# A DFT step on eight small tiles of the TensorE array instead of full matmuls with a half-empty table

## The chip, the cores and the metric

The kernel runs on one core of a Trainium2 chip. A core has TensorE (matmuls, 128x128 array, results into PSUM banks of 512 fp32 columns), VectorE (DVE), ScalarE (ACT), GpSimd (POOL), and the DMA engines, whose transfers are issued here from SyncE (SP). The metric is the device time in microseconds (us). The kernel before takes 251.26 us, the median of three runs (250.78 to 251.49). The profile is of one further execution; its span from first to last instruction is 249.1 us.

## The reference

The input has 2048 rows (S) of 640 columns (D), in bfloat16. Two branches are mixed by a gate. Branch A is a long convolution along the rows, computed with Fourier transforms of length 4096; branch B is a mixer MLP.

```python
def _A_ref(q, k, v, shift_k, ssm_k, ssm_D):
    # k_shift: sum of four shifted copies of k times shift_k ("taps")
    kv = k_shift * v
    L = 2 * S
    kv_f = rfft(kv padded to L);  kf_f = rfft(ssm_k padded to L)
    y = irfft(kv_f * kf_f)[:S] + kv * ssm_D
    return q * y

def _B_ref(x, w1, w2, w3, w4):
    h = gelu(layernorm(x) @ w1)
    # four column groups of h shifted by 1, -1, 2, -2 rows, then
    x1 = x + hs @ w2
    return x1 + gelu(layernorm(x1) @ w3) @ w4

g = sigmoid((x * gate_w).sum(-1))
return g * a + (1 - g) * b          # x = A_q in both
```

(Written shorter than the original; what is computed is the same.)

## The kernel before

The transform of length 4096 is split into two steps. Step 1 multiplies by a small DFT matrix and leaves 128 x 2 rows per block in DRAM scratch (`S_x` for kv, `S_h` for the filter). Step 2 finishes the forward transform, `product` multiplies the two spectra as complex numbers, step 3 is the first inverse step, and step 4 the last inverse step together with the gate. Steps 2 and 3 work on 32 groups of 128 rows, four groups to a task, so there are 8 tasks for x, 8 for h, 8 products and 8 tasks of step 3.

The twiddle values of step 2 stand in a compact table `CMP[:, 0]` (128 partitions, 32 groups, 2 parts c, 32 columns). For a full 128x128 matmul they are spread into `T2`: each partition belongs to one parity j (its bit 6, that is partitions 0 to 63 or 64 to 127), and its values go into the columns of that parity; the columns of the other parity are zero. Half of `T2` is therefore zero.

```python
def scaled(ev, dst, src, a):
    if ev == "A":
        A.activation(out=dst, in_=src, func=ACT.Copy, scale=a)
    else:
        V.tensor_scalar(out=dst, in0=src, scalar1=a, scalar2=0.0, op0=ALU.mult, op1=ALU.add)

def table(which, ev):
    if "I" not in st:
        TB = main.tile([P, 2, NG, P], BF16, name="TB", tag="RT")
        st["T2"], st["I"] = TB[:, 0], TB[:, 1]
    for j in range(2):
        if which == 0:
            j and (yield)
            scaled(ev[j], st["T2"].rearrange("p g (c j k) -> p g c j k", c=2, j=2)[:, :, :, j, :], CMP[:, 0], bit(6) if j else col(8))
        else: ...                      # the same for the inverse table I

def gather(name, s):                   # four groups of scratch, 640 KB
    ax = pool("C").tile([P, 4, D], BF16, name="ax", tag="ax", bufs=3)
    ...
    SP.dma_start(out=ax[:], in_=...)

def step2(name, s, ev):
    ax = st.pop((name, s))
    dst = []
    def make(u):                       # u = 0..4: one PSUM bank of 512 columns
        box = {}
        def first():
            ps = box["ps"] = psc.tile([P, 512], F32, name="ps2", tag="c")     # ring of 4 banks
            for a, b in cuts(512 * u, 512 * u + 512):                         # cut where a group of 640 ends
                i = a // D
                PE.matmul(ps[:, a - 512 * u:b - 512 * u], lhsT=st["T2"][:, 4 * s + i, :], rhs=ax[:, i, a - i * D:b - i * D], start=True, stop=True)
        def second():
            ...                        # hs from pool "L2", tag "hp", 4 buffers, or xs from pool "C", 2 buffers
            evac(ev[u], dst[0][:].rearrange("p g d -> p (g d)")[:, 512 * u:512 * u + 512], box["ps"][:])
        return first, second
    return banks(5, make)

def product(s):
    h, x = st.pop(("hs", s)), st.pop(("xs", s))
    p2 = pool("L2").tile([P, 4, D], BF16, name="p2", tag="hp", bufs=4)
    V.tensor_tensor(out=p2[0:64], in0=x[0:64], in1=h[64:128], op=ALU.mult)
    ...                                # five VectorE operations of 2560 columns in all
```

`evac` copies a PSUM bank into SBUF on ScalarE ("A") or VectorE ("V"), letter by letter as the task's name says. Small tiles of the array are already used in two places, the gate's row and the taps:

```python
def z_rows():
    ps = psc.tile([P, 512], F32, name="psz", tag="c")
    for k in range(DC):
        for c in range(4):
            PE.matmul(ps[32 * c:32 * c + 1, :]..., lhsT=GW[:, k:k + 1], rhs=st["xt", c][:, :, k, :],
                      start=(k == 0), stop=(k == DC - 1), tile_position=(0, 32 * c))
    ...

def tap(q, ev):                        # the matmuls of its first step
            for e in range(2):
                a = slice(H * e, H * e + H)          # H = 64: two row tiles, one bank each
                PE.matmul(ps[e][:, lo:hi, :], lhsT=kt[a], rhs=st["DG"][a, 4 * k + lo - i:4 * k + hi - i, a], ...)
```

Steps 1 to 4 are interleaved with the MLP (`mlp1`, `w2`, `w3`, `w4`), whose matmuls use another ring of PSUM. Every engine's order of instructions is fixed by one long list, `ORDER`, that names task, arguments and step:

```python
ORDER = (
    "open.L1.left:0 open.A2.right:0 kv_alloc:0 load_x0.1:0 consts0:0 ..."
    ...
    "... step2.x.7.AAAAV:0 step2.x.7.AAAAV:2 scale_x1.6.V:0 step2.x.7.AAAAV:4 step2.x.7.AAAAV:1 ..."
```

Of the kernel before, what the change touches and what calls it, by code (L numbers as in the profile page):

```python
# [16 lines left out]
P = 128  # L17
S = 2048
D = 640
# [22 lines left out]
def kernel(  # L42
# [196 lines left out]
    def f4_table():  # L239

        stt(col(0), bit(1), 2.0, bit(0))
        stt(col(1), bit(2), 4.0, col(0))
        stt(col(1), col(1), -1.0, pf[:])
        ts(col(1), col(1), 0.25, 1.0)
        stt(col(1), col(0), 32.0, col(1))
# [28 lines left out]
    def i_tables():  # L274

        ts(col(12), bit(5), -1.0, 1.0)
        ts(col(18), bit(5), 2.0, 1.0)
# [4 lines left out]
        ts(ag[:], R64[:, 0:NG], 4.0, col(18))  # L282
        yield
# [15 lines left out]
    def table(which, ev):  # L299

        if "I" not in st:
            TB = main.tile([P, 2, NG, P], BF16, name="TB", tag="RT")
            st["T2"], st["I"] = TB[:, 0], TB[:, 1]
        for j in range(2):
            if which == 0:
                j and (yield)
                scaled(ev[j], st["T2"].rearrange("p g (c j k) -> p g c j k", c=2, j=2)[:, :, :, j, :], CMP[:, 0], bit(6) if j else col(8))
            else:
                j and (yield)
                scaled(ev[j], st["I"].rearrange("p g (j c k) -> p g j c k", j=2, c=2)[:, :, j], CMP[:, 1], bit(5) if j else col(12))  # L310
# [77 lines left out]
    def gather(name, s):  # L388

        ax = pool("C").tile([P, 4, D], BF16, name="ax", tag="ax", bufs=3)  # L390
# [5 lines left out]
    def step2(name, s, ev):  # L396
        ax = st.pop((name, s))
        dst = []

        def make(u):  # L400
            box = {}

            def first():
                ps = box["ps"] = psc.tile([P, 512], F32, name="ps2", tag="c")
                for a, b in cuts(512 * u, 512 * u + 512):
                    i = a // D
                    PE.matmul(ps[:, a - 512 * u:b - 512 * u], lhsT=st["T2"][:, 4 * s + i, :], rhs=ax[:, i, a - i * D:b - i * D], start=True, stop=True)  # L407

            def second():
                if not dst:  # L410
                    if name == "h":
                        dst.append(pool("L2").tile([P, 4, D], BF16, name="hs", tag="hp", bufs=4))
                    else:
                        dst.append(pool("C").tile([P, 4, D], BF16, name="xs", tag="xs", bufs=2))
                    st[name + "s", s] = dst[0]
                evac(ev[u], dst[0][:].rearrange("p g d -> p (g d)")[:, 512 * u:512 * u + 512], box["ps"][:])
# [606 lines left out]
```

## Time and profile before

| Engine | busy us | share of the span | instructions |
|---|---|---|---|
| TensorE, matmuls (PE) | 227.3 | 91% | 1637 |
| TensorE, weight loads (PEld) | 128.6 | 52% | 1637 |
| VectorE (DVE) | 212.2 | 85% | 425 |
| ScalarE (ACT) | 177.9 | 71% | 292 |
| GpSimd (POOL) | 11.3 | 5% | 26 |

The busy time of an engine is the union of its instructions' times. Matmuls overlap in the array, so the mean time of one (299 ns for step 2's) is its way through the array and not what it adds; what it adds is read from the distance of the starts. In a group's line the first shape is the stationary side (rows*columns of the array), the second the moving side. "ps<-ax,TB" is step 2 (TB holds both tables), "ps<-hs,TB" step 3; xs and hs are the spectra of kv and of the filter, p and hs on VectorE the product. The copies out of PSUM all have the line of their helper, L321 on ScalarE and L323 on VectorE.

### The profile page before, as it was taken

How to read it: one execution, taken by the hardware profiler on the slowest of the kernel's cores; microseconds unless marked ns; L12 is line 12 of the kernel's file. 1: busy time of each engine (PE TensorE's matmuls, PEld its weight loads, DVE VectorE, ACT ScalarE, POOL GpSimd, SP SyncE). 2: the span in 40 equal slices, each digit the busy share in tenths (PEclk: the TensorE clock that was granted, in tenths of full speed). 3: DMA queues.
4: the chain of work that ended last, by engine and by line, in shares of the span. 5: the costliest groups of instructions: out<-in, count | busy, mean ns of one | idle time of the engine just before them, and what ended most of it. 6: DMA issues, size and time to landing. Idle time of an engine off the chain costs nothing. (4 is left out here: it accounts for less than half of the span.)

```text
span 249.1 us, 4377 instructions
## 1 busy us (share of the span) xinstructions
PE 227.3 (91%) x1637; PEld 128.6 (52%) x1637; DVE 212.2 (85%) x425; ACT 177.9 (71%) x292; POOL 11.3 (5%) x26
## 2 busy tenths in 40 slices
PE   0746999999999999999999899999989989999994
PEld 0735564444477555444555355555544546546652
DVE  6989998549995999985899999999999997508995
ACT  5599996984699999999988958845678460144530
POOL 1003301000000100031000000000000000000000
PEclk9997999999999999999999999999999999999999
DMA  6999897968858959995997618998403953268773
GB/s 250 377 416 291 189 216 167 240 256 263 241 217 243 387 204 233 346 381 146 183 304 215 204 64 251 186 366 302 132 3 101 342 218 105 105 237 281 222 265 108
DMA packets 50980, 57.65 MB, mean 231 GB/s; under 512 B 25610, under 2 KB 42763, under 8 KB 50703
## 3 DMA queue, kind: packets, MB, share of 16 engines
q1 hardware_dynamic: 50958, 57.38, 74.5%
q8 instruction: 13, 0.21, 0.4%
q14 instruction: 9, 0.07, 0.1%
HBM read 33.77 MB, written 18.36 MB: 209 GB/s over the span
## 5 line engine op out<-in xcount | busy, mean ns | idle before, releaser
L782 PE MATMUL ps<-W,gt 128*128 128x512 bf16 (+1 forms) x384 | 56.6, 299 | 0.0
L764 PE MATMUL ps<-x1t,W 128*128 128x512 bf16 x240 | 55.1, 379 | 0.0
L782 PEld LDWEIGHTS <-gt 128*128 128x128 bf16 x384 | 30.3, 98 | 23.2 <-issue 1.1
L769 ACT ACTIVATE gt<-ps 128x1024 bf16<-128x1024 f32 x24 | 24.5, 1041 | 20.3 <-PE ps L764 20.2
L764 PEld LDWEIGHTS <-W 128*128 128x128 bf16 x240 | 23.3, 98 | 26.4 <-issue 0.3
L323 DVE CAST stg<-ps 128x512 bf16<-128x512 f32 x41 | 26.4, 683 | 5.5 <-PE ps L370 5.3
L639 PE MATMUL psm<-xt,WA 128*128 128x512 bf16 x100 | 23.4, 379 | 0.0
L407 PE MATMUL ps<-ax,TB 128*128 128x512 bf16 (+3 forms) x128 | 22.5, 299 | 0.6 <-DVE hs L323 0.4
L321 ACT CAST stg<-ps 128x512 bf16<-128x512 f32 x39 | 21.7, 602 | 1.2 <-PE ps L370 1.1
L716 PE MATMUL psw<-WA,HT 128*128 128x512 bf16 (+1 forms) x116 | 21.6, 299 | 0.0
L321 ACT CAST gs<-ps 128x512 bf16<-128x512 f32 x29 | 15.2, 599 | 7.5 <-PE ps L446 7.5
L321 ACT CAST xs<-ps 128x512 bf16<-128x512 f32 x27 | 14.7, 617 | 7.0 <-PE ps L407 5.0
L321 ACT CAST hs<-ps 128x512 bf16<-128x512 f32 x27 | 14.2, 601 | 3.2 <-PE ps L407 3.2
L407 PEld LDWEIGHTS <-TB 128*128 128x128 bf16 x128 | 11.6, 98 | 9.2 <-issue 1.9
L784 DVE SCALAR_TENSOR_TENSOR X<-ps,OMG,X 128x640 bf16<-128x640 f32 x16 | 14.0, 877 | 2.4 <-PE ps L782 2.4
L718 DVE SCALAR_TENSOR_TENSOR X<-psw,X 128x640 bf16<-128x640 f32 x16 | 13.1, 819 | 3.3 <-PE psw L716 3.3
L522 PE MATMUL psk<-DG,KT 64*128 64x256 bf16 (+3 forms) x190 | 11.1, 250 | 5.0 <-ACT yk L530 3.7
L815 DVE SCALAR_TENSOR_TENSOR q<-ps,GS,q 128x320 bf16<-128x320 f32 x15 | 7.8, 542 | 9.0 <-PE ps L805 9.0
L639 PEld LDWEIGHTS <-WA 128*128 128x128 bf16 x100 | 9.5, 98 | 11.5 <-issue 0.7
L809 ACT ACTIVATE y<-ps,GS 128x320 bf16<-128x320 f32 x17 | 8.1, 525 | 9.7 <-PE ps L805 7.3
L716 PEld LDWEIGHTS <-HT 128*128 128x128 bf16 x116 | 10.1, 98 | 9.5 <-issue 0.7
L642 ACT ACTIVATE HT<-psm 128x1024 bf16<-128x1024 f32 (+1 forms) x12 | 10.5, 888 | 6.1 <-PE psm L639 5.9
(147 smaller groups left out, 386.3 us busy)
## 6 DMA issues: line engine op xcount, KB each, us to landing
S_x<-stg SPq DMA_DIRECT2D x8, 640.0 KB, 4.3
ax<-S_x SPq DMA_DIRECT2D x8, 640.0 KB, 5.3
S_h<-stg SPq DMA_DIRECT2D x8, 640.0 KB, 9.0
ax<-S_h SPq DMA_DIRECT2D x8, 640.0 KB, 5.3
S_g<-gs SPq DMA_DIRECT2D x8, 640.0 KB, 5.7
W<-in_B_w_dram SPq DMA_DIRECT2D x2, 1920.0 KB
KV<-in_A_v_dram SPq DMA_DIRECT2D x4, 640.0 KB, 11.6
gin<-S_g SPq DMA_DIRECT2D x4, 640.0 KB, 6.5
```

The source lines that it names most:

```text
L321: A.copy(out=dst, in_=src)
L323: V.tensor_copy(out=dst, in_=src)
L407: PE.matmul(ps[:, a - 512 * u:b - 512 * u], lhsT=st["T2"][:, 4 * s + i, :], rhs=ax[:, i, a - i * D:b - i * D], start=True, stop=True)
L522: PE.matmul(ps[e][:, lo:hi, :], lhsT=kt[a], rhs=st["DG"][a, 4 * k + lo - i:4 * k + hi - i, a], start=(i == 0), stop=(i == 7))
L639: PE.matmul(ps[:, v, :].rearrange("p (a b) -> p a b", a=4), lhsT=W1N[:, k, 160 * f:160 * f + P] if f < 4 else W1M[:, k, :], rhs=xt[:, :, k ...
L642: A.activation(out=st["HT"][:, 4 * c:4 * c + 4, 2 * u:2 * u + nf, :].rearrange("p t f b -> p f t b"), in_=ps[:].rearrange("p f (t b) -> p ...
L716: PE.matmul(ps[:, o:o + w], lhsT=h_tile(f, t1), rhs=W2P[:, f, o:o + w], start=(f == 0), stop=(f == 4))
L718: V.scalar_tensor_tensor(out=X1[:, t1, :], in0=ps[:], scalar=1.0, in1=X[:, t1, :], op0=ALU.mult, op1=ALU.add, accum_out=S12[:, 0, t1:t1 + 1])
L764: PE.matmul(ps[:, u, :].rearrange("p (a b) -> p a b", a=4), lhsT=st["W3"][:, k, f * P:(f + 1) * P], rhs=xt[:, :, k, :], start=(k == 0), st ...
L769: A.activation(out=gt[:, 2 * (fp % 2):2 * (fp % 2) + 2, :], in_=ps[:], func=ACT.Gelu_apprx_tanh)
L782: PE.matmul(ps[:, o:o + w], lhsT=st["gt", c, f // 4][:, f % 4, i * P:(i + 1) * P], rhs=st["W4"][:, f, o:o + w], start=(f == 0), stop=(f == ...
L784: V.scalar_tensor_tensor(out=X1[:, t1, :], in0=ps[:], scalar=OMG[:, t1:t1 + 1], in1=X1[:, t1, :], op0=ALU.mult, op1=ALU.add)
```

## The change

Step 2 no longer uses `T2`. A matmul with 64 rows and 32 columns is placed on one of eight tiles of the array: row tile j (partitions 64j to 64j+63), column tile 64c + 32o. Two groups, o = 0 and 1, share the four column tiles, so that one set of eight small matmuls covers two groups, straight from the compact table. Each parity j has its own PSUM bank. A task therefore takes eight groups (two gathers) and fills ten banks; there are 4 tasks for x and 4 for h. The groups come out in another order, which is set right in the inverse table, in the place of step 3's results in scratch, and in the last table. The spectra of x now lie in a tile `XS` of four parts, in the place that the tables had; the fourth buffer for `ax`, and a place of its own for `p2`, come from the room that `T2` leaves. The `ORDER` of all engines, and with it the engine that each copy goes to, was drawn up anew for these tasks.

```diff
     def f4_table():
         ...
+        stt(col(1), bit(3), 2.0, col(1))
+        stt(col(1), bit(4), -2.0, col(1))
         ...
     def i_tables():
-        ts(col(18), bit(5), 2.0, 1.0)
+        ts(col(18), bit(5), 4.0, 1.0)
         ...
+        odd = ag[:].rearrange("p (i j) -> p i j", j=2)[:, :, 1]
+        ts(odd, odd, -2.0, op0=ALU.add)
     def table(which, ev):
-        (T2 and I in one tile TB; which == 0 spreads CMP[:, 0] into T2, twice)
+        st["I"] = pool("C").tile([P, NG, P], BF16, name="I")
+        for o in range(2):
+            o and (yield)
+            scaled(ev[o], st["I"].rearrange("p g (j c k) -> p g j c k", j=2, c=2)[:, :, o], CMP[:, 1], bit(5) if o else col(12))
     def gather(name, s):
-        ax = pool("C").tile([P, 4, D], BF16, name="ax", tag="ax", bufs=3)
+        ax = pool("C").tile([P, 4, D], BF16, name="ax", tag="ax", bufs=4)
-    def step2(name, s, ev):
-        ax = st.pop((name, s))
+    def step2(name, b, ev):
+        ax = [st.pop((name, 2 * b + h)) for h in range(2)]
         def make(u):
+            ps = []
             def first():
-                ps = box["ps"] = psc.tile([P, 512], F32, name="ps2", tag="c")
-                for a, b in cuts(512 * u, 512 * u + 512):
-                    i = a // D
-                    PE.matmul(ps[:, a - 512 * u:b - 512 * u], lhsT=st["T2"][:, 4 * s + i, :], rhs=ax[:, i, a - i * D:b - i * D], start=True, stop=True)
+                for j in range(2):
+                    ps.append(psc.tile([P, 512], F32, name="ps2", tag="c"))
+                for lo, hi in cuts(512 * u, 512 * u + 512):
+                    i = lo // D
+                    for o in range(2):
+                        for c in range(2):
+                            for j in range(2):
+                                q, r = H * c + 32 * o, slice(H * j, H * j + H)
+                                PE.matmul(ps[j][q:q + 32, lo - 512 * u:hi - 512 * u], lhsT=CMP[r, 0, 8 * b + 2 * i + o, c, :],
+                                          rhs=ax[i // 2][r, 2 * (i % 2) + o, lo - i * D:hi - i * D], start=True, stop=True, tile_position=(H * j, q))
-            def second():
+            def second(j):
                 ...
+                        st["XS"] = main.tile([P, 4, 4, D], BF16, name="XS", tag="RT")
+                        t = st["XS"][:, (2 * b + j) % 4]
-                evac(ev[u], dst[0][:]...[:, 512 * u:512 * u + 512], box["ps"][:])
-            return first, second
+                evac(ev[2 * u + j], dst[j]...[:, 512 * u:512 * u + 512], ps[j][:])
+            return first, lambda: second(0), lambda: second(1)
     def product(s):
-        p2 = pool("L2").tile([P, 4, D], BF16, name="p2", tag="hp", bufs=4)
+        p2 = ring.tile([P, 4, D], BF16, name="p2", tag="HM", bufs=1)
     def step3(s, ev):
-        (lhsT=st["I"][:, 4 * s + i, :]; results at 4 * s * P * D, groups side by side)
+        (lhsT=st["I"][:, 8 * (s // 2) + 2 * i + s % 2, :]; results at (8 * (s // 2) + s % 2) * P * D, every second group)
     def h_shift(c):
-        (HW and HM: two tiles)
+        (HW and HM: two parts of one tile, whose place p2 takes later)
     ORDER = (
-        ... 1034 steps
+        ... 1002 steps, all in a new order
```

## The prediction

> **What bounds the kernel now.** I read the table of engines first, then busy time in four stretches, then the groups of instructions of the third stretch, then the chain that ended last.
>
> ```profile
> PE 227.3 (91%) x1637; PEld 128.6 (52%) x1637; DVE 212.2 (85%) x425; ACT 177.9 (71%) x292; POOL 11.3 (5%) x26
> ```
>
> TensorE and VectorE are both near full on average, so neither alone is "the" bound. The stretches end where the forward transforms of step 2 begin (111.7 us), where the first product begins (123.0), where the last product ends (208.5), and at the end:
>
> ```profile
> core 0: us, PE busy (x) PEld busy (x) DVE busy (x) ACT busy (x) POOL busy (x), PEclk, DMA share, GB/s
> 0.00:111.70 111.70, 97.37 (x806) 57.44 (x807) 95.04 (x274) 95.74 (x156) 9.89 (x24) 0.98 0.87 273
> 111.70:123.00 11.30, 11.17 (x70) 6.00 (x69) 7.79 (x15) 11.27 (x19) 1.38 (x2) 1.00 0.80 167
> 123.00:208.50 85.50, 81.84 (x505) 43.40 (x503) 83.38 (x78) 58.20 (x97) 0.00 (x0) 1.00 0.69 207
> 208.50:249.10 40.60, 36.92 (x261) 21.72 (x258) 26.04 (x60) 12.69 (x22) 0.00 (x0) 1.00 0.55 187
> ```
>
> In the third stretch VectorE is busy 83.4 of 85.5 us and TensorE 81.8: TensorE has little slack there, VectorE hardly any. In the fourth TensorE alone is full. The chain says the same: VectorE from 136 to 198 us, TensorE from there to 245.
>
> ```profile
> DVE 23%; PE 18%; issue 2%; ACT 0%; ACTq 0%; DVEq 0%
> ```
>
> The groups that the change touches, over the whole span:
>
> ```profile
> L407 PE MATMUL ps<-ax,TB 128*128 128x512 bf16 (+3 forms) x128 | 22.5, 299 | 0.6 <-DVE hs L323 0.4
> L323 DVE CAST hs<-ps 128x512 bf16<-128x512 f32 x13 | 8.5, 684 | 0.2
> L323 DVE CAST xs<-ps 128x512 bf16<-128x512 f32 x13 | 8.5, 683 | 3.4 <-PE ps L407 3.4
> L297 DVE TENSOR_SCALAR TB<-CMP,BF 128x2048 bf16<-128x2048 bf16 x2 | 1.4, 746 | 0.0
> ```
>
> **What small tiles cost here.** Two parts of the kernel before already use them: the gate's row (four column tiles) and the shift taps (two row tiles). Three lines of the timeline:
>
> ```profile
> 46.31 0.81 PE L639 MATMUL psm<-xt,WA 128*128 128x512 bf16 x3
> 47.05 1.25 PE L650 MATMUL psz<-xt,GW 128*1 128x512 bf16 x20
> 48.23 0.39 PE L370 MATMUL ps<-KV,F 128*128 128x512 bf16 x1
> ```
>
> Twenty 512-column matmuls take 1.25 us to the end of the last. In the start times of the trace the first four begin within 10 ns, and the sets begin 215 to 216 ns apart, which is also the distance of two full 128x512 matmuls (median start to start 216; 162 for 384 columns, 109 for 256, 55 to 56 for 128). So one set of small tiles costs what one full matmul costs, and its weight loads disappear behind the set before. The taps show it for row tiles: two start 3 to 5 ns apart, and pairs follow each other at 106 to 109 ns for 256 columns.
>
> The same lines show a price. Three full matmuls from 46.31 on would be through the array by 46.96, but the first small one starts at 47.05; five sets would be through by 48.13, the next full one starts at 48.23. Entering and leaving a tile mode costs some 0.09 to 0.10 us each (92 to 97 ns at the nine changes in the trace that are not hidden by another wait).
>
> **What the Trainium skill says.** "TensorEngine Tiling (Array Packing)", section Key Properties: tiles load and multiply in parallel, but a change of tiling mode drains the engine. The trace agrees with both (sets of 216 ns; 92 to 97 ns a change). The same page, PSUM Bottleneck: tiling speeds up TensorE and not the emptying of PSUM. That bears on this kernel: 80 banks leave step 2 before and after, at 0.68 us on VectorE or 0.60 to 0.62 on ScalarE. The same page, Restrictions and Gotchas: row tiles may not share a PSUM bank at one time (the change gives each j its own bank), and column tiling switches the fast weight load off. For the last no run here shows a number: the gate's weights have one column, the new ones 32.
>
> **The change, part by part.**
>
> TensorE, step 2. Before: 16 tasks of 8 matmuls, two each of 512, 384, 256 and 128 columns: 2 x (216 + 162 + 109 + 56) = 1.09 us, 17.4 us in all. (The 22.5 of the group is larger because it counts each matmul's way through the array.) After: 8 tasks with the same cuts, each cut a set of eight small matmuls, so 8 x 1.09 = 8.7 us if a set costs what a full matmul costs. Saved: 8.7 us. In the changed kernel's order of instructions the sets stand in 21 unbroken runs of one to four pairs of banks, so 42 changes of mode x 0.094 = 3.9 us are added. The changed schedule also turns one more block of x through TensorE (20 transposes at 55 ns, 1.1 us). Net on TensorE: -8.7 + 3.9 + 1.1 = -3.7 us.
>
> VectorE. The forward table goes (2 x 0.746 = 1.5 us). The whole order was drawn up anew, and with it the split between VectorE and ScalarE. By kinds: two row statistics fewer (-2.3), three taps moved (-0.8), six copies of step 1 fewer (-4.1), three rows normalized more in each of the two norms (+2.6), one scaling more (+0.4), three transposed blocks emptied (an estimate from ScalarE's 1.03 and 0.63 us for the same: +3), four copies more in step 2 (30 for 26, +2.7), four fewer in step 3 (-2.7), the table (-1.5), small things +0.5. Sum: about -2 us of 212. ScalarE gains about as much.
>
> The third stretch matters more than the sum. From its first product to its last VectorE now holds 25 copies out of PSUM, 8 gated sums of the MLP, 40 product operations, 3 norms and 2 scalings: 25 x 0.683 + 8 x 0.877 + 40 x 1.487 + 2.1 = 85.7 us, and the stretch took 85.5. After it holds 16 copies, 8 sums, 40 products, 1 norm, 4 scalings: 10.9 + 7.0 + 59.5 + 2.0 = 79.4 us. TensorE's part there falls from 80.6 (by start-to-start distances) to 71.9 plus some 2.5 of mode changes. So VectorE bounds it still, at about 79.2 us.
>
> The second stretch takes that back in part. Step 2 now works two old tasks at a time, and three of the new tasks' transforms instead of three old ones stand ahead of the first product. Between the first transform and the first product: ScalarE 22.3 us, VectorE 20.4, TensorE 19.9 plus 1.5 of changes, where it was 10.9, 8.0 and 11.3. Against that the first stretch loses 7.5 us of TensorE work (83.5 for 91.0), so it should end near 104.
>
> Sum: 104.2 + 22.3 + 79.2 + 40.6 (the fourth stretch holds the same 36.1 us of TensorE work in both) = 246.3 us of span, 2.8 less than 249.1. The other way of counting, TensorE's own sum with its idle time unchanged, gives 3.7 less. I take 3.6 off the measured 251.26, as the new order was made for the new costs and may overlap the edges of the stretches: 247.6 us.
>
> **Rivals.** (a) *Small weight loads are not hidden.* Weight loads of 32 columns without the fast path might pass one by one. With 28 ns for one (an estimate from the taps, whose 64-column pairs follow each other at 24 to 28 ns with two loads between, if those two shared the time) 512 of them are 14 us, 5.6 above the 8.7: the gain on TensorE is gone, and the time stays at 249 to 253. For it: nothing in this trace loads eight tiles of 32 columns. Against: two row tiles with 128-column weights hide theirs even behind 64 columns. (b) *VectorE takes the bound wholly.* Products and copies don't shrink, TensorE's gain becomes idle time, and only the moved copies help: 248 to 250. For it: 83.4 of 85.5 us. (c) *Two banks at a time starve the ring.* Step 2 and step 3 share four PSUM banks; a unit now needs two free ones, and runs of three or four units need up to eight in turn, each freed after 0.6 to 0.7 us, while a set of 512 columns takes 0.22. TensorE would stand inside a run, where before a matmul of the MLP stood between. Worth 0.2 to 0.4 us a run, 4 to 8 us at worst, of which VectorE's bound hides most: 248 to 252. (d) *The new order is simply better*, with less idle TensorE before 40 us (26.6 busy of 40 now): 243 to 245.
>
> **Range and chances.** Central 247.6. Rivals (b) and (c) put it up to 250.8, (d) down to 244. Faster by over 2% (under 246.2) needs the full 3.7 and a better fit besides: 0.25. Slower by over 2% (over 256.3) needs serial small tiles, which the gate's row speaks against: 0.05.
>
> **What would show it.** Right: the step-2 sets start 216 ns apart for 512 columns with eight starts inside some 25 ns; 42 gaps of 0.09 to 0.10 us where runs begin and end; products from first to last in 78 to 80 us with VectorE over 97% busy; the first product later than 123 us; the last stretch near 40.6. Wrong: sets spaced wider than one full matmul (rival a), waits of step-2 matmuls for copies above 3 us in sum (rival c; 0.6 now), or a product stretch whose VectorE shows idle time over 5 us.

## Result: 242.87 us, and the profile after

The changed kernel takes 242.87 us (median of four runs, 241.75 to 244.53) where the kernel before takes 251.02 beside it: a ratio of 0.968, 95% interval 0.962 to 0.975. It is 8.2 us faster; 3.6 were predicted, and the time lies below the predicted range of 244 to 250.8 us. The profile has a span of 240.0 us for 249.1.

The engines of the changed kernel, and its four stretches, cut at the same events as those of the kernel before (columns as there):

```profile
PE 224.6 (94%) x2041; PEld 122.6 (51%) x2041; DVE 209.6 (87%) x428; ACT 176.0 (73%) x300; POOL 11.1 (5%) x26
```

```profile
0.00:99.60 99.60, 90.31 (x791) 54.81 (x791) 89.20 (x259) 90.52 (x155) 7.33 (x20) 1.00 0.90 285
99.60:120.40 20.80, 20.80 (x274) 9.03 (x274) 17.67 (x44) 19.96 (x35) 3.75 (x6) 1.00 0.89 274
120.40:199.70 79.30, 78.12 (x748) 38.62 (x747) 77.65 (x69) 51.77 (x87) 0.00 (x0) 1.00 0.66 187
199.70:240.00 40.30, 35.38 (x238) 20.20 (x235) 25.04 (x57) 13.71 (x24) 0.00 (x0) 1.00 0.62 202
```

Set beside the prediction's sum:

| stretch | before | predicted | after | TensorE idle before, after |
|---|---|---|---|---|
| to the first step-2 matmul | 111.9 | 104.2 | 99.6 | 14.3, 9.3 |
| to the first product | 11.1 | 22.3 | 20.8 | 0.1, 0.0 |
| to the last product | 85.5 | 79.2 | 79.3 | 3.7, 1.2 |
| to the end | 40.6 | 40.6 | 40.3 | 3.7, 4.9 |

(Idle is the stretch less the union of the matmuls' times in the trace. The first cut of the kernel before lies 0.2 us later than in the prediction's table.) Three stretches came out within 1.5 us. Of the 6.3 us between the predicted span (246.3) and the measured one, 4.6 are in the first, which ends before the first small tile of step 2 runs. The engine line says the same in another way: TensorE's busy time fell by 2.7 us (227.3 to 224.6), its idle time by 6.4 (21.8 to 15.4).

Step 2's groups, and a piece of TensorE's timeline with small tiles between full matmuls (start, time covered, and what ran):

```profile
L413 PE MATMUL ps<-ax,CMP 64*32 64x512 bf16 (+3 forms) x512 | 13.4, 300 | 0.1
L322 DVE CAST XS<-ps 128x512 bf16<-128x512 f32 x21 | 13.4, 683 | 3.4 <-PE ps L413 3.3
L322 DVE CAST hs<-ps 128x512 bf16<-128x512 f32 x9 | 6.1, 685 | 0.4 <-PE ps L413 0.3
```

```profile
98.63 1.03 PE L776 MATMUL ps<-x1t,W 128*128 128x512 bf16 x4
99.59 0.63 PE L413 MATMUL ps<-ax,CMP 64*32 64x512 bf16 x24
100.15 2.33 PE L776 MATMUL ps<-x1t,W 128*128 128x512 bf16 x10
102.41 0.85 PE L413 MATMUL ps<-ax,CMP 64*32 64x384 bf16 x32
103.19 2.33 PE L776 MATMUL ps<-x1t,W 128*128 128x512 bf16 x10
```

512 small matmuls are busy 13.4 us where 128 full ones were 22.5, and they wait 0.1 us in sum. By start times, the eight of a set start within 22 to 24 ns in 58 of the 64 sets (the other six are spread wider, over 62 to 382 ns), and within a run sets of 384, 256 and 128 columns are followed by the next at the distance of full matmuls (162, 109 and 56 ns). After the first set of a run the next one comes some 10 ns later than that (226 ns for 512 columns).

The chain that ended last spends most of its time on TensorE, with VectorE second:

```profile
PE 40%; DVE 32%; ACT 18%; DMA 4%; issue 4%; SPq 0%; DVEq 0%
```

This chain reaches back to the first load; that of the kernel before begins at 136 us, so the shares of the two can't be compared.

Where the 4.6 us were is seen in the first 40 us. TensorE of the kernel before, its ScalarE in the same microseconds, and then TensorE of the changed kernel (in brackets the idle time before the group and what ended it):

```profile
15.61 1.52 PE L522 MATMUL psk<-DG,KT 64*128 64x256 bf16 x32 [0.25 <-ACT KT L321]
20.20 0.27 PE L522 MATMUL psk<-DG,KT 64*128 64x256 bf16 x1 [3.07 <-ACT yk L530]
```

```profile
15.84 1.24 ACT L221 ACTIVATE CMP<-n,NPI 128x1024 bf16<-128x1024 int32 x1
16.89 0.81 ACT L608 ACTIVATE jk<-X 128x640 bf16<-128x640 bf16 x1
...
18.55 1.13 ACT L221 ACTIVATE CMP<-n,NPI 128x1024 bf16<-128x1024 int32 x1
19.59 1.53 ACT L530 CAST yk<-psk 128x512 bf16<-128x512 f32 x3
```

```profile
14.28 1.52 PE L534 MATMUL psk<-DG,KT 64*128 64x256 bf16 x32 [0.25 <-ACT KT L320]
16.05 2.01 PE L534 MATMUL psk<-DG,KT 64*128 64x256 bf16 x44 [0.24 <-ACT yk L542]
```

Before the change TensorE has filled four banks with taps and stands for 3.07 us, because ScalarE makes the table's sines (L221) and the statistics of rows (L608) before it copies the taps out (L530). After that gap the trace shows TensorE's clock at half from 21.5 to 24.9 us, which costs some 1.7 us more (an estimate, half of the 3.41 us). The changed kernel has neither. It makes both tables much later (their four sines stand at 72 to 85 us) and has the first rows' statistics done by 12.2 us. And v, with which the taps are multiplied, is there earlier: the second quarter that the first taps need lands at 14.89 us, in the kernel before at 19.24 (landings here and below are the last update of the load's semaphore in the trace).

### The profile page after: what moved, and what is told of

The parts are those of the page before. It is cut to its first block, busy times and chain, and to the rows that moved or that the text cites. A ratio compares the mean times of both kernels' runs of the same rounds, so it can differ in the third digit from the quotient of the medians.

```text
span 240.0 us, 5176 instructions
## 1 busy us (share of the span) xinstructions
PE 224.6 (94%) x2041; PEld 122.6 (51%) x2041; DVE 209.6 (87%) x428; ACT 176.0 (73%) x300; POOL 11.1 (5%) x26
## 4 chain that ended last, share of the span: by engine, by line
PE 40%; DVE 32%; ACT 18%; DMA 4%; issue 4%; SPq 0%; DVEq 0%
PE ps L776 13%; PE ps L794 8%; PE psm L651 7%; ACT stg L320 4%; DVE p L436 4%; DVE p L434 4%; ACT HT L346 3%; PE ps L369 3%; DVE X L796 3%; DVE hs L442 3%; DVE hs L440 3%; DVE hs L438 3%; ACT KT L320 3%; ACT jk L733 3%; DMA q<-in_A_q_dram 2%
## 5 line engine op out<-in xcount | busy, mean ns | idle before, releaser
L794 PEld LDWEIGHTS <-gt 128*128 128x128 bf16 x384 | 29.6, 98 | 24.1 <-issue 2.8
L776 PEld LDWEIGHTS <-W 128*128 128x128 bf16 x240 | 22.5, 98 | 27.5 <-issue 3.4
L320 ACT CAST stg<-ps 128x512 bf16<-128x512 f32 x45 | 25.1, 637 | 0.7 <-PE ps L369 0.7
L322 DVE CAST stg<-ps 128x512 bf16<-128x512 f32 x35 | 22.8, 685 | 3.1 <-PE ps L369 2.9
L320 ACT CAST gs<-ps 128x512 bf16<-128x512 f32 x33 | 17.4, 598 | 11.0 <-PE ps L456 10.0
L320 ACT CAST hs<-ps 128x512 bf16<-128x512 f32 x31 | 16.5, 615 | 2.5 <-PE ps L413 2.4
L322 DVE CAST XS<-ps 128x512 bf16<-128x512 f32 x21 | 13.4, 683 | 3.4 <-PE ps L413 3.3
L413 PE MATMUL ps<-ax,CMP 64*32 64x512 bf16 (+3 forms) x512 | 13.4, 300 | 0.1
L733 ACT ACTIVATE jk<-X 128x640 bf16<-128x640 bf16 x16 | 13.4, 834 | 0.0
L320 ACT CAST XS<-ps 128x512 bf16<-128x512 f32 x19 | 10.5, 606 | 3.1 <-PE ps L413 3.1
```

The lines of the kernel that those rows point to most:

```text
L320: A.copy(out=dst, in_=src)
L322: V.tensor_copy(out=dst, in_=src)
L413: PE.matmul(ps[j][q:q + 32, lo - 512 * u:hi - 512 * u], lhsT=CMP[r, 0, 8 * b + 2 * i + o, c, :], rhs=ax[i // 2][r, 2 * (i % 2) + o, lo - i ...
L733: A.activation(out=jk[:], in_=X1[:, t1, :], func=ACT.Square, accum_out=S12[:, 1, t1:t1 + 1])
L776: PE.matmul(ps[:, u, :].rearrange("p (a b) -> p a b", a=4), lhsT=st["W3"][:, k, f * P:(f + 1) * P], rhs=xt[:, :, k, :], start=(k == 0), st ...
L794: PE.matmul(ps[:, o:o + w], lhsT=st["gt", c, f // 4][:, f % 4, i * P:(i + 1) * P], rhs=st["W4"][:, f, o:o + w], start=(f == 0), stop=(f == ...
```

## The experiments

The theory when the runs began: small tiles bring what the starts say, and the rest comes from the new order of the early part. The rivals: the tiles themselves bring more than counted; or the unloading of VectorE does. "Order" below is the list that fixes every engine's instructions. "Head" is everything up to the first matmul of `w2`.

| run | what | median us | ratio to before, 95% interval |
|---|---|---|---|
| e1_full | after, step 2 on full matmuls | 245.30 | 0.978 (0.972 to 0.985) |
| e2_twice | after, each set of tiles twice | 250.66 | 0.999 (0.997 to 1.002) |
| e3_newhead | before, with the head of after | 251.95 | 1.004 (1.002 to 1.007) |
| e4_oldhead | after, with the head of before | 251.54 | 1.002 (0.999 to 1.005) |
| e5_tapsfirst | before, taps' copies first, sines 25 us later | 259.64 | 1.034 (1.028 to 1.040) |
| e6_tableearly | after, inverse table as early as in before | 250.51 | 0.997 (0.994 to 1.001) |
| e7_copiesA | after, 15 copies from VectorE to ScalarE | 242.45 | 0.966 (0.962 to 0.970) |
| e8_turnD | after, one block of x turned by DMA | 253.68 | 1.012 (1.008 to 1.015) |
| e9_newearly | before, with all of after's order up to step 2 | 253.60 | 1.011 (1.007 to 1.015) |
| e10_oldcopiesA | before, 25 copies from VectorE to ScalarE | 244.99 | 0.980 (0.973 to 0.986) |
| e11_jam | before, taps' copies ahead of sines, within 4 us | 255.44 | 1.019 (1.010 to 1.029) |
| e12_jamcopies | e11 and e10 together | 250.47 | 0.998 (0.995 to 1.001) |
| e13_fullcopies | e1 and e7 together | 244.98 | 0.977 (0.969 to 0.984) |
| e14_vfirst | before, v loaded first | 252.67 | 1.007 (1.005 to 1.009) |
| e15_vjam | e14 and e11 together | 254.25 | 1.013 (1.009 to 1.017) |
| e16_vjamcopies | e15 and e10 together | 249.40 | 0.994 (0.991 to 0.996) |
| e17_vlate | after, v loaded late as in before | 247.18 | 0.986 (0.981 to 0.991) |
| e18_three | before, three early waits undone, and e10 | 247.75 | 0.987 (0.982 to 0.993) |

(Medians and ratios leave out executions that were over 1.5% slower than the fastest of the same kernel; with them the medians of e2, e3 and e4 are 250.88, 252.11 and 252.91.)

Ten of the eighteen came out beyond every range that was given for them beforehand: e10 was faster, and e2, e3, e4, e5, e6, e8, e9, e11 and e12 were slower. All of these but e2 and e10 change the early order.

### What the tiles bring: e1, e2, e13

e1 puts one full matmul per bank in the place of eight small ones, all else as in the changed kernel. Its stationary side is the inverse table, so the numbers are not the reference's; shapes and order are.

```diff
-for o, c, j: PE.matmul(ps[j][q:q + 32, ...], lhsT=CMP[r, 0, 8 * b + 2 * i + o, c, :], rhs=ax[i // 2][r, 2 * (i % 2) + o, ...], tile_position=(H * j, q))
+for j:       PE.matmul(ps[j][...], lhsT=st["I"][:, 8 * b + 2 * i + j, :], rhs=ax[i // 2][:, 2 * (i % 2) + j, ...])
```

> The changed kernel with its own order, but step 2 on full 128x128 matmuls (stationary side taken from the inverse table, so that the numbers of step 2 are not those of the reference): 128 full matmuls for 512 small ones, no change of mode. Theory A (the early part of the new order is what the prediction missed; the tiles are worth their sum on TensorE and no more): TensorE work rises by 8.7 - 3.9 = 4.8 us, of which what lies in the product stretch is hidden behind VectorE (77 of 79 us); step 2 to first product lengthens by about 2 us; time 243 to 246. Theory B (the tiles themselves, with the buffers they free, brought the whole gain): time 249 to 251. First stretch (to the start of step 2) unchanged at 99.6 in both.

It took 245.30 us, 2.4 more than the changed kernel. Its first three stretches:

```profile
0.00:101.30 101.30, 90.02 (x788) 54.74 (x789) 89.17 (x259) 90.41 (x155) 7.31 (x20) 1.00 0.90 281
101.30:123.20 21.90, 21.90 (x130) 11.55 (x129) 17.93 (x43) 20.16 (x35) 3.58 (x6) 1.00 0.97 282
123.20:202.70 79.50, 79.50 (x504) 42.95 (x503) 77.64 (x69) 51.87 (x87) 0.00 (x0) 1.00 0.58 177
```

The first stretch, in which no tile of step 2 runs, is 1.7 us longer only because the first load of k landed at 8.40 us and not at 6.58; that moment differs from profile to profile. TensorE is busy 79.50 of 79.50 us in the third. So with full matmuls, but all else as in the changed kernel, 5.8 us of the 8.2 are kept. This is more than the new order alone: the forward table, which is no longer spread, and the buffers in its room are kept too.

e2 issues every set of eight twice, the same result twice.

```diff
+for rep in range(2):
     (the eight matmuls of a set)
```

> The changed kernel with every set of eight small matmuls issued twice (the second overwrites the first; the output stays as it was). 512 more small matmuls, no more changes of mode. If a set costs one full matmul: TensorE work rises by 8.7 us, 3.9 more than with full matmuls in the same places, so the pair of runs measures the changes of mode where TensorE is the bound. Theory A: 244 to 248, not above 2 us over the run with full matmuls. If the second set's weight loads were not hidden, or issue were the limit, sets would stand further apart than 216 ns for 512 columns.

Its second and third stretch:

```profile
99.60:123.00 23.40, 22.39 (x460) 10.96 (x460) 17.94 (x44) 20.51 (x35) 3.58 (x6) 1.00 0.92 261
123.00:206.60 83.60, 83.60 (x1065) 43.12 (x1065) 78.34 (x69) 51.95 (x87) 0.00 (x0) 1.00 0.58 169
```

7.8 us more than the changed kernel, for 8.7 us of added sets, with TensorE full in the third stretch: a set costs what was counted (two sets of 512 columns that follow each other inside a run start 216 ns apart), and TensorE's sum goes into the time nearly whole. The range given beforehand, 244 to 248, was missed, as TensorE had only 1.2 us idle in the third stretch of the changed kernel and so little of the added work could be hidden.

e13 is e1 with the 15 copies of e7 (below) on ScalarE.

```diff
 (e1)
-step2.x.1.AVVAAAAAVA ... (15 letters V)
+step2.x.1.AAAAAAAAAA ...
```

> The changed kernel with 15 copies of the product stretch on ScalarE, as in an earlier run (242.45), and step 2 on full matmuls (from the inverse table, so the numbers of step 2 are not the reference's). VectorE no longer bounds any stretch, so the whole price of full matmuls should show: 17.4 us for 8.7 plus 5.1 of mode changes, 3.6 less the part that was already waiting: 245 to 246.5. If something else bounds: 243.

244.98 us, against 242.45 for e7 with tiles: 2.5 us. Two pairs of kernels agree on 2.4 to 2.5 us by their medians, and in both pairs the slowest execution with tiles is faster than the fastest without. Part of it can be the first load: in the profiles, counted from the first matmul of step 2 on, e1 is 2.4 us longer than the changed kernel and e13 1.4 longer than e7. So the tiles bring 1.4 to 2.5 us.

### Who bounds the product stretch: e7, e10

Copies out of PSUM between the first and the last product go from VectorE to ScalarE, 15 in the changed kernel, 25 in the kernel before.

```diff
 (e7, on after)
-step2.x.1.AVVAAAAAVA ...
+step2.x.1.AAAAAAAAAA ...
 (e10, on before)
-step2.h.1.AVAAA ...
+step2.h.1.AAAAA ...
```

> The changed kernel with 15 copies out of PSUM in the product stretch moved from VectorE to ScalarE (all copies there of steps 2 and 3 but those of the last task). VectorE has 10 us less in that stretch, ScalarE 9 more (27.5 idle there now). If VectorE bounds the stretch, as the prediction had it: 79.3 falls to 75 or less, time 238.5 to 240.5. If TensorE bounds it (1.2 us idle, and the run with doubled sets grew by 8.0 of 8.7): 78 to 79, time 242 to 243.5.

> The kernel before with all 25 copies out of PSUM of steps 2 and 3 in the product stretch (but those of the last task) moved from VectorE to ScalarE. VectorE has 17 us less there, ScalarE 15 more of 27.3 idle. If VectorE bounds that stretch in the kernel before, as the prediction read it: 85.5 falls to 81 to 82, TensorE's own sum there, time 246.5 to 248. If TensorE bounds it together with ScalarE: 84 to 86, time 250 to 251.5.

The third stretch of each, e7 first:

```profile
120.80:197.60 76.80, 76.18 (x723) 37.81 (x729) 67.79 (x53) 59.07 (x103) 0.00 (x0) 1.00 0.65 187
197.60:239.60 42.00, 36.18 (x252) 21.24 (x252) 24.93 (x58) 13.70 (x24) 0.00 (x0) 1.00 0.61 205
```

```profile
121.90:203.70 81.80, 81.69 (x513) 43.96 (x512) 68.02 (x53) 69.62 (x122) 0.00 (x0) 1.00 0.71 214
```

In the kernel before, VectorE did bound this stretch: relieved of 15 us it has 13.8 us of slack, TensorE becomes full (81.69 of 81.80), the stretch is 3.7 us shorter (81.8 for 85.5), and the time falls by 5.4 us. (In the profile the last stretch is 1.0 us shorter too, and the first 1.1, where the first load landed 1.7 us earlier.) In the changed kernel the same relief shortens the stretch by 2.5 us, the last stretch gives 1.7 back, and the time is not to be told from the changed kernel's. So after the change both engines are busy within 1.7 us of the whole stretch.

### The heads exchanged: e3, e4, e9

```diff
 (e3: ORDER of before)
-(before's steps up to the first w2 matmul)
+(after's steps up to there; unfinished early tasks woven into what follows)
 (e4: the reverse)
 (e9: ORDER of before: after's order of everything ahead of step 2, then a bridge for both tables and four w3 blocks)
```

> The kernel before (forward table, full matmuls) with the changed kernel's order from the start to the first matmul of the second projection, and its own order from there; what was open at that point is woven in one by one. Theory A: TensorE's idle time before step 2 falls from 14.3 to about 9.5 us, step 2 starts some 4 to 5 us earlier than 111.7, and the time is 245.5 to 248. Theory B: 250 to 251.5, the head by itself brings nothing.

> The changed kernel (small tiles) with the order of the kernel before up to the first matmul of the second projection, its own order from there. Theory A: TensorE idles some 14 us before step 2, step 2 starts at 103 to 105 and not at 99.6, time 246 to 249. Theory B: 242 to 244.

> The kernel before (forward table, full matmuls, its own tasks) with everything up to the start of step 2 in the changed kernel's order, a short bridge for the tables and four blocks of the MLP that the kernel before has there, and its own order from its first step-2 matmul on. Cleaner than the first run of this kind, whose seam lay at 55 to 80 us and cost 2.7 us of waits. If the early order by itself makes the gain and the tiles only their 2.4 us: TensorE idle before step 2 about 9 to 11 us (14.3 before), no stretch at half clock before step 2, time 245 to 247.5. If the early order only pays with the small tiles behind it: 250 to 252.

The old head on the new kernel (e4) takes the whole gain away, with the 3.07 us gap at 17 us and 3.4 us of half clock after it as in the kernel before, but also with gaps of 0.93 and 2.52 us where the orders are joined (84 and 93 us) and another 3.4 us of half clock from 95.6. The new head on the old kernel (e3, e9) doesn't bring it: in both the gap at 17 us is gone, but new gaps open where the orders are joined (e3: 0.73, 1.18 and 0.82 us at 75 to 82 us; e9: 2.77 us at 105.9, TensorE waiting for a gelu on ScalarE, and half clock from 109.1 to 112.5). The three are therefore inconclusive by their times. They show that the gap goes with the head: e3 and e9 are without it though they have full matmuls, T2 and the old buffers. They don't show what it is worth or which part of the head makes it.

### One cause at a time in the changed kernel: e6, e17, e8

e6 makes the inverse table as early as the kernel before does; the loads stay early.

```diff
 (ORDER of after)
+i_tables:0 i_tables:1 behind the first step of the first statistics; i_tables:2 i_tables:3 i_tables:4 ahead of the first taps' copies
-i_tables:0 ... i_tables:4 where they stood
```

> The changed kernel with the making of the inverse table moved back to where the kernel before has it: started with the first row statistics, its two sines on ScalarE ahead of the first copies of the taps. Theory A2: TensorE stands some 2 to 3.5 us near 16 us, possibly followed by 3.4 us at half clock; step 2 starts at 102 to 104 where it was 99.6; time 245 to 248. Theory A3: ScalarE's and VectorE's work that is moved away from 55 to 75 us makes up for it: 242.5 to 244.

Its ScalarE, VectorE and TensorE:

```profile
17.88 1.13 ACT L221 ACTIVATE CMP<-n,NPI 128x1024 bf16<-128x1024 int32 x1
20.56 1.15 ACT L221 ACTIVATE CMP<-n,NPI 128x1024 bf16<-128x1024 int32 x1 [1.55 <-DVE n L219]
21.62 1.54 ACT L542 CAST yk<-psk 128x512 bf16<-128x512 f32 x3
```

```profile
19.05 0.75 DVE L210 TENSOR_SCALAR n<-m,sm 128x1024 int32<-128x1024 int32 x1 [0.37 <-ACT CMP L221]
19.84 0.69 DVE L219 TENSOR_SCALAR n<-n 128x1024 int32<-128x1024 int32 x1
20.44 0.68 DVE L548 TENSOR_TENSOR KV<-psk,KV 128x512 bf16<-128x512 f32 x1
```

```profile
16.66 1.52 PE L534 MATMUL psk<-DG,KT 64*128 64x256 bf16 x32 [0.25 <-ACT KT L320]
21.18 0.37 PE L534 MATMUL psk<-DG,KT 64*128 64x256 bf16 x1 [3.00 <-DVE KV L548]
```

v is not waited for here (it landed at 17.99 us, and VectorE is at the table's integer steps until its product with v, L548, starts at 20.44), and yet the gap is back (3.00 us), with half clock from 20.6 to 27.4 us, and 7.6 of the 8.2 us are lost. In its profile the span is 8.8 us longer; 2.4 of these are a late first load (8.96 us for 6.58), which e8 has too (8.84) without this edit.

e17 changes nothing but the early loads: a quarter of x and a quarter of v not needed yet are issued ahead of the second quarter of v that the first taps multiply with.

```diff
 (ORDER of after, loads only)
-load_x.1 v_load.3 v_load.2 load_x.3 ... v_load.1 v_load.0 load_x.2
+load_x.1 v_load.3 load_x.2 v_load.0 v_load.2 load_x.3 ... v_load.1
```

> The changed kernel with only its early loads put in the order of the kernel before: one quarter of x and the unused quarter of v ahead of the second quarter of v that the first taps multiply with. Theory (an early v is needed for the gain of the first stretch): VectorE waits for v near 17 us by some 3 us, TensorE gets a gap of 2 to 3 us and half clock for 3.4 us after it, time 246 to 249. Rival (the load order does not matter in the changed kernel): as the changed kernel, 242 to 244.5.

TensorE's timeline, and then the first three stretches:

```profile
17.32 0.27 PE L534 MATMUL psk<-DG,KT 64*128 64x256 bf16 x1 [0.23 <-ACT yk L542]
19.91 2.44 PE L534 MATMUL psk<-DG,KT 64*128 64x256 bf16 x43 [2.32 <-DVE KV L548]
```

```profile
0.00:104.20 104.20, 90.70 (x787) 54.83 (x787) 89.42 (x259) 90.57 (x155) 7.31 (x20) 0.98 0.85 273
104.20:125.00 20.80, 20.80 (x274) 9.03 (x274) 17.67 (x43) 19.98 (x35) 3.75 (x6) 1.00 0.90 274
125.00:204.30 79.30, 78.11 (x747) 38.66 (x746) 77.65 (x69) 51.76 (x87) 0.00 (x0) 1.00 0.65 185
```

VectorE's product with v (L548) starts at 19.16 us after 2.91 us idle, TensorE has a gap of 2.32 us, half clock from 21.1 to 24.6, and the time is 4.3 us longer. The second and third stretch are as in the changed kernel to 0.1 us. With this one swap of loads the first stretch and the total are near the prediction's (104.2 for 104.2, 247.2 for 247.6). In this profile 1.3 us of the first stretch are a later first load (7.87 for 6.58), so the agreement is in part chance; the difference of the medians is not, as the intervals of the ratios lie apart (0.981 to 0.991, 0.962 to 0.975). The Trainium skill, "DMA: Bandwidth & Descriptors", section Queues, rings and completion order, says that each DMA engine takes a queue's descriptors in the order in which they stand in its ring. The trace agrees: the loads of 640 KB land in the order of their issue, 1.6 us apart (14.34, 15.93, 17.50 and 19.09 us, the last being the v that is waited for). Two loads moved ahead of it are thus 3.2 of the 4.2 us by which it lands later than in the changed kernel (19.09 for 14.89); the rest goes with the later first load.

e8 was meant to save the 20 transposes on TensorE that the new order had added, by turning the block with a DMA transpose.

```diff
-x_turn.1.V (TensorE, VectorE)
+x_turn.1.D (DMA transpose)
```

> The changed kernel with the second block of the normalized x turned by a DMA transpose instead of 20 TensorE transposes and three VectorE copies. TensorE has 1.1 us less, VectorE 3 us less near 27 us. If TensorE's sum sets the time: 241.5 to 242.5. If the DMA transpose comes too late for the first projection: 243 to 245.

The line of TensorE's timeline that matters:

```profile
39.57 1.89 PE L651 MATMUL psm<-xt,WA 128*128 128x512 bf16 x4 [8.51 <-DMA xt<-xn]
```

The transpose came 8.5 us late, with half clock from 36.4 to 43.2 us, and the time is 10.8 us longer. The 1.1 us of transposes on TensorE buy the absence of this wait; what they cost by themselves this run does not tell.

### The same causes in the kernel before: e5, e11, e12, e14, e15, e16, e18

```diff
 (ORDER of before, from the first tap on)
 e5:  +(copies of taps 5 and 9) ahead of the statistics; i_tables:2..4 some 25 us later
 e11: +(the same copies) between the statistics and i_tables:2..4, all within 4 us
 e14: -load_x.3 load_x.2 v_load.3 v_load.0 v_load.2 ... load_x.1
      +v_load.3 v_load.2 load_x.3 load_x.1 ... load_x.2 v_load.0
 e12 = e11 + e10;  e15 = e14 + e11;  e16 = e15 + e10
 e18: e14 + e10, x_stats.0 finished ahead of k_load's last steps, x_norm.0 and taps next, x_stats.3 and i_tables:2..4 behind them
```

> The kernel before with two small moves in its order: the first taps' copies out of PSUM stand ahead of the row statistics on ScalarE, and the second half of the inverse table's making (two sines on ScalarE with their integer steps on VectorE) comes some 25 us later. Theory A2 (the early part, by this one jam: ScalarE makes tables and statistics while the taps' PSUM banks wait for it, TensorE stands for 3.07 us, and the clock is then granted at half for 3.4 us, worth 1.7 us): the gap at 17 us shrinks under 1 us, no stretch at half clock follows, step 2 starts 3 to 4.5 us earlier (107.5 to 109), time 246.5 to 248.5. Theory A3 (other work near 60 to 110 us takes the gain back, as in the run that took over the whole early part): under 1.5 us gained, 249.5 to 251.

259.64 us: the statistics now stood behind the copies, TensorE waited 4.20 us for the normalised rows, and the late sines jammed step 1 at 53 to 57 us. Half clock twice, 6.8 us each.

> The kernel before with twenty neighbouring steps of its order rearranged within about 4 us: the first taps' copies (on both engines) stand before the two sines of the inverse table and behind the row statistics. This is the jam that the changed kernel's order doesn't have, and nothing else. If the jam is what the early part of the new order avoids: TensorE's gap of 3.07 us at 17 us falls to about 1, no stretch at half clock follows it, step 2 starts 2.5 to 4 us earlier at the same landing of the first load, time 247 to 249. If some other chain then takes its place, as where the copies stood ahead of the statistics: 250 to 252.

With the copies moved by 4 us only, the gap stayed, and its releaser changed. TensorE and VectorE of e11:

```profile
20.65 1.43 PE L522 MATMUL psk<-DG,KT 64*128 64x256 bf16 x22 [3.19 <-DVE KV L536]
24.33 0.71 PE L550 MATMUL pst<-IDB,xn 128*128 128x128 bf16 x5 [2.26 <-ACT xn L591]
```

```profile
19.90 0.69 DVE L536 TENSOR_TENSOR KV<-psk,KV 128x512 bf16<-128x512 f32 x1 [4.08 <-DMA KV<-in_A_v_dram]
```

A second wait had stood beside the first all along: v landed at 19.78 us here, and in the kernel before at 19.24, just 0.35 us ahead of ScalarE's first copy (19.59).

> The same rearrangement together with the 25 copies of the product stretch on ScalarE: the kernel before, full matmuls and forward table, without the two things that cost it most. If both gains add (245.0 with the copies alone): 241.5 to 243, that is, the changed kernel's time without small tiles. If the first does nothing: 245.

250.47 us: what the copies gain in the third stretch (81.9 us, as in e10) the head loses (117.3 us to the first step-2 matmul). The two add up: 1.019 x 0.980 is 0.999, and 0.998 was measured.

> The kernel before, with only the order of its early loads changed: the two quarters of v that the first taps multiply with (rows of chunks 3 and 2) are issued ahead of the rows of x and of the quarter of v that is used later. Theory (the 3 us gap of TensorE at 17 us stands on two waits that end within half a us of each other, ScalarE's sines and statistics at 19.6 and the load of v at 19.9, so taking away either one leaves it): v is there early, yet the gap stays near 3.1 us with ScalarE as what ends it, and so does the half-clock window after it; time 249.5 to 251.5, ratio 0.994 to 1.002. Rival (the load alone holds the gap): gap under 1.5 us, no half-clock window near 21 us, time 246 to 248. Rival (loads ahead of x starve the statistics): slower, 252 or more.

v is there early (13.39 us), ScalarE still late, and the gap is longer, 4.64 us, since the taps began earlier. As a rival had it, the kernel is slower (252.67 us), with 6.8 us of half clock:

```profile
14.02 1.52 PE L522 MATMUL psk<-DG,KT 64*128 64x256 bf16 x32 [0.25 <-ACT KT L321]
20.18 2.35 PE L522 MATMUL psk<-DG,KT 64*128 64x256 bf16 x22 [4.64 <-ACT yk L530]
```

> The load order of v changed as in the run above, and also the taps' copies put ahead of the sines within 4 us, which alone made the kernel before slower (255.4) because VectorE then waited 4.08 us for v. Theory (both waits together make the gap): the gap at 17 us falls below 1 us, the half-clock window after it disappears, and the span before step 2 shortens by 3 to 5 us; time 246 to 248, ratio 0.98 to 0.99. Rival (the order of the statistics and the normalised rows is a third wait, as the later gaps of that run at 22 and 26 us say): those gaps remain, with a half-clock window after them, and the time is 250 or more.

The expectation of the theory failed, the rival's came: with both waits undone a third shows, the second statistics waiting 2.11 us for a load of x that now stands behind v, and then the normalised rows. TensorE of e15:

```profile
18.40 1.06 PE L522 MATMUL psk<-DG,KT 64*128 64x256 bf16 x22 [1.88 <-DVE KV L536]
22.09 0.71 PE L550 MATMUL pst<-IDB,xn 128*128 128x128 bf16 x5 [2.63 <-ACT xn L591]
```

> The run above with 25 copies of the product stretch moved from VectorE to ScalarE as well (alone 245.0). Theory: the two gains are in different stretches and add up, so that the kernel without small tiles comes to 240 to 243, as fast as the changed kernel or faster. Rival (the later gaps stay): 245 to 250.

249.40 us, again the copies' gain less the head's loss (1.013 x 0.980 is 0.993, measured 0.994).

> The kernel before, full matmuls and T2 as they were, with three waits of its head undone together and the copies of the product stretch shared out: the two quarters of v loaded first; the statistics of the first four rows of X finished before 12 us, while the engines still wait for data, with the normalised rows and the taps' copies directly after; the second statistics, which wait for a later load of X, and the sines behind these; and 25 copies of the product stretch on ScalarE. Theory (the gap of 17 us stands on several waits that end together, so it goes only when all are undone): no gap of TensorE over 1 us after 13 us, no half-clock window before step 2, first stretch 106 to 109 (the kernel before had 111.9), third 81.8, fourth 39.6, time 239.5 to 243, ratio 0.957 to 0.971. Rival (a further wait takes their place): a gap of 2 us or more remains, or the sines jam the tables later, first stretch 111 or more, time 245 or more.

The gap at 17 us is gone at last, but the rival came here too. A block of transposed x waits on ScalarE behind a sine, and taps wait later (1.45 us at 31.8). TensorE of e18:

```profile
24.92 4.26 PE L639 MATMUL psm<-xt,WA 128*128 128x512 bf16 x19 [2.38 <-ACT xt L321]
```

Half clock from 33.4 to 36.8, first stretch 114.2 us. 247.75 us is 2.8 us worse than the copies alone (244.99, e10). No kernel here got the first stretch of the changed kernel without taking its order whole; e1 and e13 did take it whole, without tiles, and have 101.3.

## Why the prediction was wrong, point by point

*Sets of eight cost one full matmul; loads hidden (rival a): right.* Inside a run sets start at the distance of full matmuls, and e2 pays 7.8 us for 8.7 us of sets. Loads of 32 columns take 88 to 93 ns each and pass behind the set before.

*42 changes of mode at 94 ns, 3.9 us: too low.* Entering costs 94 ns, leaving 115 to 117 measured from when the last set would be done (the eight starts of a set spread over 23 ns, which shows once per run), and between first and second set 10 ns are lost: 0.22 us per run, 4.6 for 21 runs, and 5.8 with the waits that fall on these edges. So the tiles save 8.7 - 5.8 = 2.9 us, where the prediction's terms gave 4.8; e1 and e13 measure 1.4 to 2.5. The Trainium skill, "TensorEngine Tiling (Array Packing)", section Key Properties, says only that a change of mode drains the array; these are the sizes.

*Product stretch, 79.2 us, VectorE bounds it: right in size, half right in cause.* 79.3 us, VectorE 97.9% busy. Before the change VectorE was the bound (e10). After it TensorE is as near (e2, e7), so a further relief of VectorE brought nothing in the time. The prediction put TensorE's part at 71.9 plus 2.5 us; its busy time there is 78.1. That the size came out is in part luck: with 1.2 us more of its own TensorE would have set the stretch.

*Second stretch 22.3, fourth 40.6: right within 1.5 us* (20.8, 40.3). But the 22.3 were ScalarE's sum; ScalarE is busy 19.96 us there and TensorE all 20.80. Nor did ScalarE gain what VectorE lost over the whole kernel: its busy time fell by 1.9 us (177.9 to 176.0), VectorE's by 2.6.

*Two banks at a time starve the ring (rival c): fell.* Step 2 waits 0.1 us in sum.

*The first stretch "loses 7.5 us of TensorE work (83.5 for 91.0), so it should end near 104", and TensorE's own sum "with its idle time unchanged": the step that failed.* The work did leave: busy time there fell by 7.3 us (97.6 to 90.3, of which some 1.7 are the half-clock window that is gone, so that some 5.6 are work). But the same subtraction took the idle time and the clock of the old head as given, though the whole order was new. Idle time fell by 5.0 us: 3.1 are the gap at 17 us, 1.3 an earlier first load, the rest small. So step 2 begins at 99.6 us and the first product comes at 120.4, where the prediction had it later than 123. I had seen "less idle TensorE before 40 us" and gave it as rival (d), 243 to 245, without naming a wait that would go, and against it I set nothing; that rival happened:

```profile
0.00:40.00 40.00, 26.55 (x336) 19.43 (x337) 35.20 (x109) 32.27 (x49) 6.32 (x18) 0.96 0.95 283
```

```profile
0.00:40.00 40.00, 31.77 (x368) 22.47 (x370) 37.27 (x125) 34.96 (x61) 6.00 (x18) 1.00 1.01 314
```

(The kernel before, then the changed one: TensorE is busy 5.2 us more in its first 40.)

What made that gap is shown from the changed kernel's side. Either of two things brings it back by itself: sines and table ahead of the taps' copies (e6, 7.6 us) or v behind other loads (e17, 4.3 us). Together they are more than the 8.2, since both open the same gap, so neither figure is a share of the gain. The kernel before has both, with a third behind them, so that taking one or two away there (e5, e11, e14, e15) only shows the next.

Of the 8.2 us some 2.4 are the tiles (1.4 to 2.5), and the other 5.8 are everything else: the new order, the copies that it moved, the forward table that is not spread and the buffers in its room. How they divide stays open. Copies alone bring 5.4 us in the old order (e10), and this adds up with what is done to the head (e12, e16); the gap with its half clock is some 4.8 us of the first stretch (3.07 and the estimate of 1.7); and the first load may be worth over a microsecond by itself. Not tried: a whole order drawn up anew for full matmuls with T2.

## What to carry to other kernels

When a change comes with a new order of everything, predict the parts that the change does not touch too: list the gaps over 2 us in the old trace, find for each what ends it and what would end it next, and ask whether the new order still has it. The order in which early loads are issued is part of the kernel's schedule, and v behind two loads that nobody needs yet cost more here (4.3 us) than the tiles bring (1.4 to 2.5). Small tiles pay per set, but each run of sets pays 0.22 us to get in and out, so runs should be long.

## What the runs showed of the hardware

A gap of TensorE of 2.3 to 3.1 us can be enough for half clock, which begins within the gap or soon after it: 3.4 us of it with 2.32 us (e17) and 3.07 us (before), 6.8 with 3.00 (e6). The same gap of 3.08 us as in the kernel before had 6.8 in e10. Where further gaps followed it lasted 10.2 us (e11, with gaps of 3.19, 2.26 and 1.11) and 13.7 us (e12). Gaps of 0.5 us had none, nor did 1.18 and 0.82 us close together (e3); e18's gap of 2.38 us at 22.5 had none either, while 1.45 us at 31.8, after 0.45 us just ahead of it, had 3.4. The Trainium skill, "TensorE: Matmul & The Clock Gate", Part 1 (The HAM clock gate), gives idle windows of some 3.4 us, free-running, as the cause of half clock. The length agrees, in multiples of 3.41 us; that the same gap may or may not bring it fits windows that run freely; but gaps shorter than such a window sufficed.

The first load of k landed anywhere from 6.2 to 9.0 us in the profiles of these kernels, also where the instructions ahead of it were the same (6.58 us in the changed kernel, 6.60 in e2, 8.40 in e1, 8.46 in e13). There is one profile of each kernel, so whether this is chance or belongs to the kernel is not shown. A difference of a microsecond in the first stretch of two single profiles says nothing.
